# Row differences of a Winograd input transform by accumulating DMAs instead of VectorE subtractions

## The chip, the core and the metric

The kernel runs on one NeuronCore of a Trainium2 chip. TensorE (PE) multiplies matrices and writes its sums to PSUM; VectorE (DVE), ScalarE (ACT) and GpSimd (POOL) work elementwise; SyncE (SP) issues the loads and stores. ScalarE and GpSimd can issue DMAs too. The metric is the device time of one execution in microseconds. Lower is better. The time before is the median of three runs.

## What is computed

A residual block of a diffusion network, in bf16, on an input of 2 images x 512 channels x 64 x 64:

```
def gn(z, gamma, beta):            # group norm, 4 groups of 128 channels
    ...
h = conv3(_silu(gn(x, g1, be1)), w1)          # 3x3 convolution, 512 -> 512
h = h + (_silu(t_emb) @ w_emb).reshape(B, C, 1, 1)
h = conv3(_silu(gn(h, g2, be2)), w2)
return x + h
```

The two 3x3 convolutions are nearly all of the work.

## The kernel before

**Tiling.** Each convolution is one "layer" (0 and 1). A layer is cut into four chunks, (b, ch): two images and, in each, two halves of 32 rows. For each chunk the kernel computes four output tiles `ot` of 128 channels; one (chunk, ot) is called a group here, so there are 16 groups in a layer and 32 in all. The rows go through a Winograd transform F(4,3): six transformed row positions stand for four output rows. Of these positions 0, 5, 3 and 4 take three column taps each ("direct", L670), and positions 1 and 2 are transformed along the columns as well ("nested", L681). A group is thus 24 matmuls into `mid` (positions 3 and 4), 24 into two `acc` banks (positions 0 and 5) and 32 shorter ones into `nst`. The last chunk of layer 1 treats positions 3 and 4 as nested too.

**The input transform** is made by the generator `produce_V` (L374). For each chunk it handles four units, one for each 128 input channels `ct`, so there are 32 units in all. A unit takes these steps:

- SP loads 34 rows (L389), except in the very first chunk, whose image already lies in SBUF.
- ScalarE applies the group norm and SiLU into `a_tmp` (L396), one of two buffers, of 36 rows of 66 columns; GpSimd clears the border row (L383 or L385).
- ScalarE writes 4 times the rows into planes 1 to 4 of `kt` (L408). After this the generator yields.
- VectorE makes the row differences in `kt`: L410, L411 and L412 with 1056 elements in each partition, and L414 with 528. The generator yields again.
- VectorE makes V from `kt`: L428 and two times L437 for the rows, then L448 and two times L453 for the columns.

There is one `kt` tile (`kt_main`). Only the first chunk alternates between two (`kt_two`). So L408 of the next unit has to wait until L437 of this unit has read `kt`.

**The output side of a group.** ScalarE moves `nst` from PSUM into `rm` (L716, twice) and `mid` too (L731). VectorE combines them (L723 to L725, then L738 to L747) into `tt`. In the groups that do not end on VectorE, TensorE adds `tt` into the `acc` banks with two matmuls against a scaled identity (L755), and ScalarE writes the result (L764). This end of a group is issued only after the nested matmuls of the next group. In the groups of `DVE_ENDS` VectorE does it instead (L761). ScalarE also takes the sums for the second group norm (L772, L774) and scales most of the weights (L239), whose transform VectorE finishes (L236); the weights of layer 0 are prepared during its first chunk and those of layer 1 around the boundary of the layers.

**What sets the order.** The program is written by groups, and a small planner (`_Background`) steps the generators of V and of the weights between the matmul sets, by their deadlines. A scheduling layer then orders the instructions on each engine by its own estimate of when each becomes ready. Each engine runs its queue in that order, so that an instruction which waits holds up everything behind it on its engine. GpSimd's queue before holds only memsets of `a_tmp` and the small power operations of the group norm (L174, L176, L181).

Of the kernel before, what the change touches and what calls it, by code (L numbers as in the profile page):

```python
# [9 lines left out]
ACT = mybir.ActivationFunctionType  # L10
ALU = mybir.AluOpType
# [3 lines left out]
F16 = mybir.dt.float16  # L15
# [47 lines left out]
def kernel(  # L63
# [13 lines left out]
    nc = tc.nc  # L77
    P = nc.NUM_PARTITIONS
# [5 lines left out]
    WP = W + 2  # L84
# [3 lines left out]
    TH = 4  # L88
    TR = 8
    CR = TH * TR  # L90
# [4 lines left out]
    EPS = 1e-5  # L95
    WS = 64.0
    KAPPA = 1.0 / (6.0 * WS)
    ROW = TR * WP
    VD, VN = 4 * ROW, NC * 2 * NHALF
    VCT = VD + VN  # L100
    VTMP = 2 * ROW
    NMAT = 14
# [8 lines left out]
    consts = ctx.enter_context(tc.tile_pool(name="consts", bufs=1))  # L111
# [6 lines left out]
    otmp = ctx.enter_context(tc.tile_pool(name="otmp", bufs=1))  # L118
# [24 lines left out]
    a_tmp = [consts.tile([P, CR + 4, WP], F16, name=f"a_tmp{i}") for i in range(2)]  # L143
    for at in a_tmp:
        nc.gpsimd.memset(at[:, :, 0:WP:WP - 1], 0.0)
    kt_main = consts.tile([P, TR, 7, WP], F16, name="kt")

    gparm = consts.tile([4 * CT, P], BF16, name="gparm")
    tparm = consts.tile([B * ET, P], BF16, name="tparm")
# [5 lines left out]
    def flat(t):  # L155
        return t[:].rearrange("p r w -> p (r w)")
# [187 lines left out]
    def new_V():  # L344
        return vpool.tile([P, CT * VCT + VTMP], F16, tag="V", name="V")

    def v_direct(V, ct):
        return V[:, ct * VCT:ct * VCT + VD].rearrange("p (s t w) -> p s t w", s=4, w=WP)

    def v_nested(V, ct):  # L350
        return V[:, ct * VCT + VD:(ct + 1) * VCT].rearrange("p (c q n) -> p c q n", c=NC, q=2)
# [4 lines left out]
    def v_nested34(V, ct, c):  # L356
        if c < 2:
            t = V[:, ct * VCT:ct * VCT + 4 * NHALF]
        else:
            t = more["V"][:, ct * 4 * NHALF:(ct + 1) * 4 * NHALF]  # L360
        return t.rearrange("p (c q n) -> p c q n", c=2, q=2)
# [12 lines left out]
    def produce_V(layer, b, ch, resident=None, V=None, kts=(kt_main,)):  # L374
        if V is None:
            V = new_V()
        Vt[(layer, b, ch)] = V
        r0 = ch * CR - 1
        lo, hi = max(r0, 0), min(r0 + CR + 2, H)
        for ct in range(CT):  # L380
            at, kt = a_tmp[ct % 2], kts[ct % len(kts)]
            if ch == 0:
                nc.gpsimd.memset(at[:, 0, 1:W + 1], 0.0)  # L383
            if ch == NCH - 1:
                nc.gpsimd.memset(at[:, CR + 1, 1:W + 1], 0.0)  # L385
            if resident is None:
                src = srcp.tile([P, CR + 2, W], BF16 if layer == 0 else F16, tag="src")
                src_dram = x_v[b, ct] if layer == 0 else h_scr[b, ct]
                nc.sync.dma_start(  # L389
                    out=src[:, lo - r0:hi - r0, :],  # L390
                    in_=src_dram[:, lo * W:hi * W].rearrange("p (r w) -> p r w", w=W),
                )
                sap = src[:, lo - r0:hi - r0, :]
            else:
                sap = resident[ct][:, lo:hi, :]
            nc.scalar.activation(  # L396
                out=at[:, lo - r0:hi - r0, 1:W + 1], in_=sap,
                func=ACT.Silu, bias=nb_all[:, layer, b, ct:ct + 1],
                scale=sc_all[:, layer, b, ct:ct + 1],
            )  # L400

            def rows(j, n):
                return at[:, j:j + CR, :].rearrange("p (t f) w -> p t (f w)", f=TH)[:, :, 0:n * WP]

            def planes(j, n):
                return kt[:, :, j:j + n].rearrange("p t f w -> p t (f w)")

            nc.scalar.activation(out=planes(1, 4), in_=rows(0, 4), func=ACT.Copy, scale=4.0)  # L408
            yield
            nc.vector.tensor_tensor(out=planes(5, 2), in0=planes(3, 2), in1=planes(1, 2), op=ALU.subtract)  # L410
            nc.vector.tensor_tensor(out=planes(2, 2), in0=planes(2, 2), in1=rows(3, 2), op=ALU.subtract)  # L411
            nc.vector.tensor_tensor(out=kt[:, :, 1:5:3], in0=at[:, 4:4 + CR].rearrange("p (t f) w -> p t f w", f=TH)[:, :, 0:2],  # L412
                                    in1=at[:, 2:2 + CR].rearrange("p (t f) w -> p t f w", f=TH)[:, :, 0:2], op=ALU.subtract)
            nc.vector.tensor_scalar(out=kt[:, :, 0], in0=kt[:, :, 6], scalar1=0.5, scalar2=None, op0=ALU.mult)  # L414
            yield
            Vc = v_direct(V, ct)
            vt = V[:, CT * VCT:].rearrange("p (q t w) -> p q t w", q=2, w=WP)

            four = (layer, b, ch) == FOUR
            if four:  # L420
                vt2 = stage.tile([P, 2, TR, WP], F16, tag="stage", name="vt2")

            def pair(k):
                s = Vc[:, k].rearrange("p t w -> p (t w)")
                return bass.AP(tensor=s.tensor, offset=s.offset,
                               ap=[list(s.ap[0]), [vt[:, k].offset - s.offset, 2], [1, ROW]])

            nc.vector.tensor_tensor(out=Vc[:, 2:4], in0=kt[:, :, 1:5:3].rearrange("p t f w -> p f t w"),  # L428
                                    in1=kt[:, :, 5:7].rearrange("p t f w -> p f t w"), op=ALU.subtract)
            in0 = kt[:, :, 1:4:2].rearrange("p t f w -> p f t w")  # L430
            in1 = kt[:, :, 0:3:2].rearrange("p t f w -> p f t w")
            for k, op in enumerate((ALU.add, ALU.subtract)):
                if four:
                    for i, o in enumerate((vt2[:, k], vt[:, k])):
                        nc.vector.tensor_tensor(out=o, in0=in0[:, i], in1=in1[:, i], op=op)
                else:
                    nc.vector.tensor_tensor(out=pair(k).rearrange("p q (t w) -> p q t w", w=WP), in0=in0, in1=in1,  # L437
                                            op=op)

            def columns(rows2, lo2, hi2):  # L440
                vrow = rows2.rearrange("p q t w -> p (q t) w")

                def plane_pair(o, step):
                    r = vrow[:, :, o:o + HALF]
                    return bass.AP(tensor=r.tensor, offset=r.offset,
                                   ap=[list(r.ap[0]), list(r.ap[1]), [step, 2], [1, HALF]])

                nc.vector.tensor_tensor(  # L448
                    out=lo2.rearrange("p c q (t w) -> p (q t) c w", w=HALF),
                    in0=plane_pair(0, HALF + 2), in1=plane_pair(1, HALF), op=ALU.subtract)  # L450
                ev, od = vrow[:, :, HALF + 1:W + 1], vrow[:, :, 1:HALF + 1]
                for c, (i0, i1, op) in enumerate(((ev, od, ALU.add), (od, ev, ALU.subtract))):
                    nc.vector.tensor_tensor(out=hi2[:, c].rearrange("p q (t w) -> p (q t) w", w=HALF),  # L453
                                            in0=i0, in1=i1, op=op)

            Vn = v_nested(V, ct)
            columns(vt, Vn[:, 0:2], Vn[:, 2:4])
            yield
            if four:
                columns(vt2[:], v_nested34(V, ct, 0), v_nested34(V, ct, 2))  # L460
# [12 lines left out]
    for i, prm in enumerate((g1, be1, g2, be2)):  # L473
        nc.scalar.dma_start(
            out=gparm[CT * i:CT * (i + 1), :],
            in_=prm.rearrange("(ct p) -> ct p", p=P),
# [42 lines left out]
        me_gram(me[:, 1], b0[:, 0:P])  # L519
        gn_scale_bias(b0, me, 0, 0, ct, 1)  # L520

    kt_two = otmp.tile([P, TR, 7, WP], F16, tag="rm", name="kt_two")
    gen_V0 = produce_V(0, 0, 0, resident=x0_res, V=V0, kts=(kt_main, kt_two))
    def two_banks(ct):
        if ct % 2 == 0:
# [52 lines left out]
    for layer in range(2):  # L578
        for idx, (b, ch) in enumerate(chunks):
            for ot in range(CT):  # L580
# [41 lines left out]
                rows = slice(ch * CR * W, (ch + 1) * CR * W)  # L622

                ssum = ssq = None
                if layer == 1:
                    xr = stg.tile([P, CR, W], BF16, tag="io")
                    nc.sync.dma_start(
                        out=xr[:], in_=x_v[b, ot][:, rows].rearrange("p (r w) -> p r w", w=W))
# [13 lines left out]
                accs = {}  # L642
# [60 lines left out]
                rm = otmp.tile([P, 2, CR * W], F16, tag="rm")  # L703
# [10 lines left out]
                def evac_nested(k=0):  # L714
                    for bank in range(2):
                        nc.scalar.activation(  # L716
                            out=raw[:, bank].rearrange("p q t e w -> p (q t e w)"),
                            in_=accs["nst", k][bank][:].rearrange("p q t e w -> p (q t e w)"), func=ACT.Copy,
                            scale=(KAPPA, 0.5 * KAPPA)[bank])

                def cols_mid(k=0):
                    m1, m2 = raw[:, 1, :, :, 0], raw[:, 1, :, :, 1]
# [7 lines left out]
                def evac_mid():  # L730
                    i_a = nc.scalar.activation(  # L731
                        out=msl[:, 0:4:2].rearrange("p s t w -> p s (t w)"),
                        in_=accs["mid"][:].rearrange("p s t e w -> p s (t e w)"), func=ACT.Copy, scale=KAPPA)
                    if not first_evac:
                        first_evac.append(i_a)

# [172 lines left out]
```

## Time and profile before

| What | Value |
|---|---|
| median of 3 runs | 515.71 us (515.32 to 516.96) |
| the profiled execution | 513.87 us |
| its span, first to last instruction | 512.0 us |
| mean granted TensorE clock | 0.985 |
| PE busy | 487.2 us, 3184 matmuls |
| DVE busy | 445.0 us, 1008 instructions |
| ACT busy | 345.8 us, 351 instructions |
| POOL busy | 16.8 us, 56 instructions |
| DMA | 59.87 MB, of which q1 59.32 MB with 34.7% of 16 engines |

Busy time is the time in which an engine had an instruction running. A row of the groups of instructions gives the line, the engine, the operation, the tiles (out<-in), the shapes (partitions x elements), the count, then busy us and mean ns of one, then the idle time of the engine ahead of it and what ended that idle time. A row of the DMA issues gives the tiles, the queue, the count, the size of one in KB and the median time from issue to landing. The views by stretch give the busy us of each engine in a window of the span, the granted clock, the DMA share and GB/s.

### The profile page before, as it was taken

Reading aid. Unit: us, or ns where it says so; the run is one execution under the profiler, and the core shown is the slowest. Engines: PE = TensorE matmul, PEld = TensorE weight load, DVE = VectorE, ACT = ScalarE, POOL = GpSimd, SP = SyncE. Lnnn points to the kernel's source line nnn. Section 1 sums busy time; section 2 is a strip of 40 time slices with the busy share of each in tenths; the row PEclk is TensorE's granted clock in tenths of the full one; section 3 lists DMA queues with packets and bytes.
Section 4 is the critical chain, followed back from the end, with each engine's and each line's share of the span. In section 5 each row is a group of like instructions: output and inputs, shape, how many; then the busy total and the mean of one; then the engine's idle time right before and its main releaser. Section 6 shows DMA issues by size and latency. Waiting matters only on the chain.

```text
span 512.0 us, 8257 instructions
## 1 busy us (share of the span) xinstructions
PE 487.2 (95%) x3184; PEld 288.1 (56%) x3184; DVE 445.0 (87%) x1008; ACT 345.8 (68%) x351; POOL 16.8 (3%) x56
## 2 busy tenths in 40 slices
PE   4898899899999999999899999999999999999996
PEld 4766655355555555555454555554555555557784
DVE  4899999999956896378799999987999999987876
ACT  4776999999976964487999998339665353113350
POOL 1210000100000000000000000010000000000000
PEclk9689999999999999999999999999999999999999
DMA  8949312322332221134543813224434311222212
GB/s 310 362 153 308 93 58 84 114 96 83 107 108 91 100 72 42 43 125 109 181 119 101 251 64 130 78 83 140 153 114 137 107 45 55 83 92 76 82 42 84
DMA packets 22996, 59.87 MB, mean 117 GB/s; under 512 B 2091, under 2 KB 11435, under 8 KB 22571
## 3 DMA queue, kind: packets, MB, share of 16 engines
q1 hardware_dynamic: 22896, 59.32, 34.7%
q8 instruction: 25, 0.41, 0.3%
q14 instruction: 16, 0.13, 0.1%
q10 hardware_dynamic: 59, 0.01, 0.0%
HBM read 42.54 MB, written 16.78 MB: 116 GB/s over the span
## 4 chain that ended last, share of the span: by engine, by line
PE 29%; DVE 16%; ACT 4%; issue 2%; POOL 0%; DVEq 0%; ACTq 0%
PE acc L670 10%; PE nst L681 10%; PE mid L670 7%; DVE U L236 2%; DVE V L437 2%; ACT S L239 1%; PE half L670 1%; DVE sts L738 1%; DVE kt L410 1%; DVE S L236 1%; DVE V L428 1%; DVE V L453 1%; DVE kt L411 1%; ACT junk L774 1%; DVE V L448 1%
## 5 line engine op out<-in xcount | busy, mean ns | idle before, releaser
L670 PE MATMUL acc<-V,R 128*128 128x512 f16 x744 | 171.2, 386 | 1.2 <-ACT yst L764 1.2
L670 PE MATMUL mid<-V,U 128*128 128x512 f16 x672 | 157.2, 387 | 2.9 <-ACT rm L716 1.6
L670 PEld LDWEIGHTS <-R 128*128 128x128 bf16 x792 | 77.1, 98 | 92.5 <-issue 1.8
L681 PE MATMUL nst<-V,U 128*128 128x256 f16 x1088 | 124.8, 273 | 0.2 <-DVE U L236 0.2
L681 PEld LDWEIGHTS <-U 128*128 128x128 f16 x1120 | 109.5, 98 | 21.2 <-DVE U L236 0.7
L670 PEld LDWEIGHTS <-U 128*128 128x128 f16 x672 | 65.5, 98 | 86.1 <-issue 8.3
L716 ACT ACTIVATE rm<-nst 128x1024 f16<-128x1024 f32 x72 | 72.1, 1019 | 55.1 <-PE nst L681 36.8
L396 ACT ACTIVATE a_tmp<-src,nb_all,sc_all 128x2112 f16<-128x2112 f16 (+1 forms) x28 | 60.1, 2153 | 25.2 <-DVE nb_all L335 11.5
L408 ACT ACTIVATE kt<-a_tmp 128x2112 f16<-128x2112 f16 x30 | 59.0, 1966 | 15.0 <-DVE V L437 7.8
L731 ACT ACTIVATE rm<-mid 128x1024 f16<-128x1024 f32 x28 | 28.7, 1025 | 24.9 <-PE mid L670 24.9
L437 DVE TENSOR_TENSOR V<-kt 128x1056 f16<-128x1056 f16 x52 | 36.6, 704 | 0.7
L410 DVE TENSOR_TENSOR kt<-kt 128x1056 f16<-128x1056 f16 x30 | 21.1, 703 | 11.8 <-ACT kt L408 11.7
L239 ACT ACTIVATE S<-R 128x1536 f16<-128x1536 bf16 (+1 forms) x28 | 31.1, 1168 | 0.0
L774 ACT ACTIVATE junk<-yst 128x2048 f16<-128x2048 f16 x16 | 30.7, 1917 | 0.1
L772 ACT ACTIVATE junk<-yst 128x1024 f16<-128x1024 f16 x16 | 17.0, 1060 | 19.1 <-DVE yst L747 13.0
L236 DVE TENSOR_TENSOR U<-S 128x1536 f16<-128x1536 f16 x32 | 29.7, 950 | 0.0
L723 DVE TENSOR_TENSOR tu<-rm 128x512 f16<-128x512 f16 x36 | 15.1, 420 | 15.6 <-ACT rm L716 15.5
L738 DVE TENSOR_TENSOR sts<-rm 128x1024 f16<-128x1024 f16 x32 | 21.9, 686 | 4.3 <-ACT rm L731 3.5
L453 DVE TENSOR_TENSOR V<-V 128x512 f16<-128x512 f16 x64 | 25.5, 433 | 0.0
L725 DVE TENSOR_TENSOR rm<-tu,rm 128x1024 f16<-128x1024 f16 x36 | 24.7, 686 | 0.6 <-ACT rm L716 0.2
L448 DVE TENSOR_TENSOR V<-V 128x1024 f16<-128x1024 f16 x32 | 22.5, 703 | 0.4
L239 ACT ACTIVATE S<-g1t 128x768 f16<-128x768 bf16 x28 | 22.1, 846 | 0.0
(131 smaller groups left out, 479.9 us busy)
## 6 DMA issues: line engine op xcount, KB each, us to landing
src<-h_scr SPq DMA_DIRECT2D x16, 528.0 KB, 3.9
h_scr<-yst SPq DMA_DIRECT2D x16, 512.0 KB, 2.6
xr<-in_x_dram SPq DMA_DIRECT2D x16, 512.0 KB, 3.8
out_dram<-xr SPq DMA_DIRECT2D x15, 512.0 KB, 2.8
src<-in_x_dram SPq DMA_DIRECT2D x12, 528.0 KB, 6.8
R<-in_w_dram SPq DMA_DIRECT2D x16, 384.0 KB, 3.7
xt<-in_x_dram SPq DMA_DIRECT2D x8, 512.0 KB, 4.7
g1t<-in_w_dram SPq DMA_DIRECT2D x16, 192.0 KB, 2.9
```

Of the source, the lines that this page charges most:

```text
L236: nc.vector.tensor_tensor(out=o, in0=i0, in1=i1, op=op)
L239: ts = lambda o, i, f: nc.scalar.activation(out=o, in_=i, func=ACT.Copy, scale=f)
L396: nc.scalar.activation(out=at[:, lo - r0:hi - r0, 1:W + 1], in_=sap, func=ACT.Silu, bias=nb_all[:, layer, b, ct:ct + 1], scale=sc_all[:, l ...
L408: nc.scalar.activation(out=planes(1, 4), in_=rows(0, 4), func=ACT.Copy, scale=4.0)
L437: nc.vector.tensor_tensor(out=pair(k).rearrange("p q (t w) -> p q t w", w=WP), in0=in0, in1=in1, op=op)
L448: nc.vector.tensor_tensor(out=lo2.rearrange("p c q (t w) -> p (q t) c w", w=HALF), in0=plane_pair(0, HALF + 2), in1=plane_pair(1, HALF), o ...
L453: nc.vector.tensor_tensor(out=hi2[:, c].rearrange("p q (t w) -> p (q t) w", w=HALF), in0=i0, in1=i1, op=op)
L670: nc.tensor.matmul(out, lhsT=w_direct(pos, ct, kx), rhs=rhs, start=first, stop=last)
L681: nc.tensor.matmul(accs["nst", (pos - 1) // 2][bank][:, q, :, plane, :], lhsT=lhsT, rhs=rhs.rearrange("p (t w) -> p t w", w=HALF), start=s ...
L716: nc.scalar.activation(out=raw[:, bank].rearrange("p q t e w -> p (q t e w)"), in_=accs["nst", k][bank][:].rearrange("p q t e w -> p (q t ...
L731: i_a = nc.scalar.activation(out=msl[:, 0:4:2].rearrange("p s t w -> p s (t w)"), in_=accs["mid"][:].rearrange("p s t e w -> p s (t e w)") ...
L774: nc.scalar.activation(out=junk[:], in_=yf, func=ACT.Square, scale=float(HW) ** -0.5, accum_out=ssq[:, ch:ch + 1])
```

## The change

The transform's intermediate planes are laid out anew and their signs turned. `kt` becomes two blocks of four planes. With r0 to r5 the six rows under one tile, block 1 holds T_j = r_(j+2) - 4 r_j for j = 0 to 3, and block 0 holds 2 (r1 - r3) and r2 - r4. ScalarE writes block 1 with scale -4 as one contiguous run of 2112 elements in each partition. The rows r_(j+2) are then added into it:

- in every unit but the four of the first chunk, by two accumulating DMAs from `a_tmp` into `kt`, 1056 elements of each partition apiece, issued by GpSimd;
- in the first chunk by one VectorE addition of 2112 elements.

VectorE keeps one subtraction of 1056 elements and one scaling of 528 in this step. The step that makes V has the same number of instructions with the same shapes, reading other planes. Since two planes of V come out with the opposite sign, the scales at which PSUM is read are negated.

```
+    ROWS_BY_DMA = lambda layer, b, ch: (layer, b, ch) != (0, 0, 0)
...
-    kt_main = consts.tile([P, TR, 7, WP], F16, name="kt")
+    kt_main = consts.tile([P, 2, TR, 4, WP], F16, name="kt")
...
-            nc.scalar.activation(out=planes(1, 4), in_=rows(0, 4), func=ACT.Copy, scale=4.0)
+            whole = kt[:, 1].rearrange("p t f w -> p (t f w)")
+            nc.scalar.activation(out=whole, in_=flat(at)[:, 0:CR * WP], func=ACT.Copy, scale=-4.0)
+            below = flat(at)[:, 2 * WP:(2 + CR) * WP]
+            if ROWS_BY_DMA(layer, b, ch):
+                for h in range(2):
+                    part = slice(h * CR * WP // 2, (h + 1) * CR * WP // 2)
+                    nc.gpsimd.dma_start(out=whole[:, part], in_=below[:, part], accum_op=ALU.add)
             yield
-            nc.vector.tensor_tensor(out=planes(5, 2), in0=planes(3, 2), in1=planes(1, 2), op=ALU.subtract)
-            nc.vector.tensor_tensor(out=planes(2, 2), in0=planes(2, 2), in1=rows(3, 2), op=ALU.subtract)
-            nc.vector.tensor_tensor(out=kt[:, :, 1:5:3], in0=at[:, 4:4 + CR].rearrange("p (t f) w -> p t f w", f=TH)[:, :, 0:2],
-                                    in1=at[:, 2:2 + CR].rearrange("p (t f) w -> p t f w", f=TH)[:, :, 0:2], op=ALU.subtract)
-            nc.vector.tensor_scalar(out=kt[:, :, 0], in0=kt[:, :, 6], scalar1=0.5, scalar2=None, op0=ALU.mult)
+            if not ROWS_BY_DMA(layer, b, ch):
+                nc.vector.tensor_tensor(out=whole, in0=whole, in1=below, op=ALU.add)
+            nc.vector.tensor_tensor(out=planes(0, 0, 2), in0=rows(1, 2), in1=rows(3, 2), op=ALU.subtract)
+            nc.vector.tensor_scalar(out=kt[:, 0, :, 0], in0=kt[:, 0, :, 0], scalar1=2.0, scalar2=None, op0=ALU.mult)
             yield
...
-            nc.vector.tensor_tensor(out=Vc[:, 2:4], in0=kt[:, :, 1:5:3].rearrange("p t f w -> p f t w"),
-                                    in1=kt[:, :, 5:7].rearrange("p t f w -> p f t w"), op=ALU.subtract)
-            in0 = kt[:, :, 1:4:2].rearrange("p t f w -> p f t w")
-            in1 = kt[:, :, 0:3:2].rearrange("p t f w -> p f t w")
+            T4 = kt[:, 1].rearrange("p t f w -> p f t w")
+            nc.vector.tensor_tensor(out=Vc[:, 2:4], in0=T4[:, 2:4], in1=T4[:, 0:2], op=ALU.subtract)
...
+            in0, in1 = both(1, 2), both(0, 1)
...
-                            scale=(KAPPA, 0.5 * KAPPA)[bank])
+                            scale=(-KAPPA, -0.5 * KAPPA)[bank])
...
-                        in_=accs["mid"][:].rearrange("p s t e w -> p s (t e w)"), func=ACT.Copy, scale=KAPPA)
+                        in_=accs["mid"][:].rearrange("p s t e w -> p s (t e w)"), func=ACT.Copy, scale=-KAPPA)
```

More of the change, by code (lines that the diff above doesn't have):

```diff
@@ L403, in rows, with planes @@
                 return at[:, j:j + CR, :].rearrange("p (t f) w -> p t (f w)", f=TH)[:, :, 0:n * WP]
-            def planes(j, n):
-                return kt[:, :, j:j + n].rearrange("p t f w -> p t (f w)")
-            nc.scalar.activation(out=planes(1, 4), in_=rows(0, 4), func=ACT.Copy, scale=4.0)
-            yield
-            nc.vector.tensor_tensor(out=planes(5, 2), in0=planes(3, 2), in1=planes(1, 2), op=ALU.subtract)
-            nc.vector.tensor_tensor(out=planes(2, 2), in0=planes(2, 2), in1=rows(3, 2), op=ALU.subtract)
-            nc.vector.tensor_tensor(out=kt[:, :, 1:5:3], in0=at[:, 4:4 + CR].rearrange("p (t f) w -> p t f w", f=TH)[:, :, 0:2],
-                                    in1=at[:, 2:2 + CR].rearrange("p (t f) w -> p t f w", f=TH)[:, :, 0:2], op=ALU.subtract)
-            nc.vector.tensor_scalar(out=kt[:, :, 0], in0=kt[:, :, 6], scalar1=0.5, scalar2=None, op0=ALU.mult)
+            def planes(k, j, n):
+                return kt[:, k, :, j:j + n].rearrange("p t f w -> p t (f w)")
+            whole = kt[:, 1].rearrange("p t f w -> p (t f w)")
[5 more added lines that the diff above has]
+                    nc.gpsimd.dma_start(out=whole[:, part], in_=below[:, part], accum_op=ALU.add)
+            yield
+            if not ROWS_BY_DMA(layer, b, ch):
+                nc.vector.tensor_tensor(out=whole, in0=whole, in1=below, op=ALU.add)
+            nc.vector.tensor_tensor(out=planes(0, 0, 2), in0=rows(1, 2), in1=rows(3, 2), op=ALU.subtract)
+            nc.vector.tensor_scalar(out=kt[:, 0, :, 0], in0=kt[:, 0, :, 0], scalar1=2.0, scalar2=None, op0=ALU.mult)
             yield
@@ L426, in pair, with both @@
                                ap=[list(s.ap[0]), [vt[:, k].offset - s.offset, 2], [1, ROW]])
-            nc.vector.tensor_tensor(out=Vc[:, 2:4], in0=kt[:, :, 1:5:3].rearrange("p t f w -> p f t w"),
-                                    in1=kt[:, :, 5:7].rearrange("p t f w -> p f t w"), op=ALU.subtract)
-            in0 = kt[:, :, 1:4:2].rearrange("p t f w -> p f t w")
-            in1 = kt[:, :, 0:3:2].rearrange("p t f w -> p f t w")
+            T4 = kt[:, 1].rearrange("p t f w -> p f t w")
+            nc.vector.tensor_tensor(out=Vc[:, 2:4], in0=T4[:, 2:4], in1=T4[:, 0:2], op=ALU.subtract)
+            def both(d, t):
+                o = kt[:, 1, :, t].offset - kt[:, 0, :, d].offset
+                v = kt[:, 0, :, d]
+                return bass.AP(tensor=v.tensor, offset=v.offset,
+                               ap=[list(v.ap[0]), [o, 2]] + [list(e) for e in v.ap[1:]])
+            in0, in1 = both(1, 2), both(0, 1)
             for k, op in enumerate((ALU.add, ALU.subtract)):
@@ L520, in stats0 @@
         gn_scale_bias(b0, me, 0, 0, ct, 1)
-    kt_two = otmp.tile([P, TR, 7, WP], F16, tag="rm", name="kt_two")
+    kt_two = otmp.tile([P, 2, TR, 4, WP], F16, tag="rm", name="kt_two")
     gen_V0 = produce_V(0, 0, 0, resident=x0_res, V=V0, kts=(kt_main, kt_two))
```

## The prediction

> **What bounds the kernel now.** I read the page's busy times first, then TensorE's time by stretch, then who made TensorE wait, then the rows of the instructions that the change touches.
>
> ```profile
> PE 487.2 (95%) x3184; PEld 288.1 (56%) x3184; DVE 445.0 (87%) x1008; ACT 345.8 (68%) x351; POOL 16.8 (3%) x56
> ```
>
> TensorE is busy for 95% of the span, so VectorE's 87% is not the bound by itself. What VectorE can give back is only the time in which TensorE waits for it. The view by stretch shows where that is (columns: window and its length, then busy us of PE, PEld, DVE, ACT and POOL, clock, DMA share, GB/s).
>
> ```profile
> 46.00:130.00 84.00, 79.19 (x508) 45.15 (x506) 81.70 (x176) 77.57 (x89) 3.06 (x9) 1.00 0.32 106
> 130.00:246.00 116.00, 116.00 (x680) 64.37 (x679) 85.47 (x205) 82.77 (x91) 3.00 (x9) 1.00 0.30 94
> 246.00:365.00 119.00, 114.09 (x640) 62.42 (x639) 111.75 (x241) 95.99 (x101) 2.95 (x10) 1.00 0.38 124
> 365.00:503.00 138.00, 138.00 (x853) 83.36 (x852) 126.17 (x276) 57.98 (x51) 0.70 (x4) 1.00 0.25 85
> ```
>
> From 130 to 246 us and from 365 to 503 us TensorE has no gap at all. It idles for 84.00 - 79.19 = 4.8 us in the first stretch and 119.00 - 114.09 = 4.9 us in the third, together 9.7 us. These are the stretches in which VectorE is nearly full (81.70 of 84.00 and 111.75 of 119.00). Ahead of 46 us the first chunk is prepared, which the DMAs do not touch. TensorE's waits after 46 us name the causes:
>
> ```profile
> PE acc L755 <- DVE tt L740: 2.3, 2, 1.7
> PE acc L755 <- DVE tt L742: 1.9, 2, 1.7
> PE mid L670 <- ACT rm L716: 1.6, 1, 1.6
> PE acc L755 <- DVE tt L744: 1.4, 4, 0.7
> PE acc L670 <- ACT yst L764: 1.2, 2, 0.9
> ```
>
> Eight waits at L755, 2.3 + 1.9 + 1.4 = 5.6 us, are for `tt` from VectorE; the rest is mostly ScalarE's. So the change can win at most 9.7 us, and 5.6 us if it only speeds up VectorE.
>
> **What is removed.** These rows bear on it:
>
> ```profile
> L408 ACT ACTIVATE kt<-a_tmp 128x2112 f16<-128x2112 f16 x30 | 59.0, 1966 | 15.0 <-DVE V L437 7.8 <-DVE V L435 6.6 <-DVE var L173 0.6
> L410 DVE TENSOR_TENSOR kt<-kt 128x1056 f16<-128x1056 f16 x30 | 21.1, 703 | 11.8 <-ACT kt L408 11.7
> L411 DVE TENSOR_TENSOR kt<-kt,a_tmp 128x1056 f16<-128x1056 f16 x30 | 21.2, 706 | 0.5
> L412 DVE TENSOR_TENSOR kt<-a_tmp 128x1056 f16<-128x1056 f16 x30 | 21.0, 701 | 0.0
> L428 DVE TENSOR_TENSOR V<-kt 128x1056 f16<-128x1056 f16 x30 | 21.0, 701 | 0.5 <-PE acc L670 0.5
> L453 DVE TENSOR_TENSOR V<-V 128x512 f16<-128x512 f16 x64 | 25.5, 433 | 0.0
> ```
>
> In 28 units two of the three subtractions go: 28 x 2 x 0.70 = 39 us of VectorE, 1.4 us a unit. Of these, units 4 to 10 (counted from 0) lie in the first stretch and units 18 to 25 in the third. In the four units of the first chunk, one addition of 2112 elements takes the place of two of 1056. It is not in the trace: it costs at least one row of L410, 0.70 us, and at most two, 1.41 us. I take 1.23 us, since 544 elements more make L410 0.27 us longer than L453, so 1056 more make 0.70 + 0.52. That is 0.2 us less a unit, under 1 us in all, and counts as nothing beside the open points. ScalarE's copy keeps its 2112 elements; written contiguously it lies between L774's 1.92 us for 2048 and the present 1.97 us, so 0 to -0.05 us a unit. The sign changes are constants of existing instructions and cost nothing.
>
> **What is added: a DMA's latency between ScalarE's copy and VectorE.** In each of the 28 units V's first instruction (L428 before) now waits for two accumulating DMAs. They wait for the copy, are issued one after the other by GpSimd, and together carry 128 x 2112 x 2 bytes = 528 KB of `a_tmp`, and must read the same amount of `kt` before they write it. No row shows an accumulating DMA or one issued by GpSimd. The nearest are:
>
> ```profile
> src<-h_scr SPq DMA_DIRECT2D x16, 528.0 KB, 3.9
> h_scr<-yst SPq DMA_DIRECT2D x16, 512.0 KB, 2.6
> src<-in_x_dram SPq DMA_DIRECT2D x12, 528.0 KB, 6.8
> ...
> g1t<-in_w_dram SPq DMA_DIRECT2D x16, 192.0 KB, 2.9
> ```
>
> From below: the pair lands no faster than the store's 2.6 us with a free issue. From above: the two run one after the other at the slow load's 6.8 us each, 13.6 us, plus two issues. For an issue the longest GpSimd row is L181 with 1.04 us and the shortest a 0.2 us memset; I take 1 us. I take the load of the same 528 KB, 3.9 us, behind two issues, with the second read beside the first: **latency 5.9 us**, ends 2.6 and 15.7 us.
>
> By the Trainium skill (DMA: Bandwidth & Descriptors, section "Anatomy of one DMA") a DMA from GpSimd takes about 2.0 us plus bytes over 436 GB/s, an estimate of 2.6 us for each half, and 3.2 us if the pair overlaps fully; the rows agree on the order of size (2.6 and 3.9 us for about 512 KB). With that the latency would be 4 to 5 us, and the sum below would come out close to no change. The skill's page SBUF — State Buffer, section "Who interferes with whom", speaks against the change: VectorE instructions in a two-port mode shut GpSimd out of SBUF, and so hold up the descriptors of its DMAs. No row of this trace shows it.
>
> **What covers it.** In the timeline of ScalarE and VectorE I took, for each unit, the time from the end of L408 to the start of L428. For units 4 to 10 it is 8.6, 9.1, 4.5, 2.4, 3.1, 3.5 and 2.5 us; for units 18 to 25 it is 2.2, 3.1, 18.5, 17.9, 3.7, 3.4, 3.5 and 4.7 us; in the other 13 it lies between 2.4 and 17.4 us. Relative to before, VectorE is late by latency minus this margin (the 1.4 us that go are inside the margin, so it is early by at most 1.4 us). At 5.9 us the short margins leave it late by 1.2 to 3.7 us, in 11 of those 15 units.
>
> VectorE's queue is in order, so what stands behind the waiting instruction matters. In the built program the waits of units 6, 10, 22 and 25 stand behind the group's `tt` work, and TensorE's L755 is safe. In units 7, 18, 19, 23 and 24 work that frees `rm` or makes `tt` (L723 to L742) stands right behind. Their lateness is 3.5, 3.7, 2.8, 2.5 and 2.4 us, mean 3.0. Units 8 and 9 are alike, but TensorE has no gap from 112 to 130 us, and a group has slack there: from the end of `mid` to L755 lie 24 `acc` and 32 `nst` matmuls, 5.34 + 3.49 = 8.8 us in the chain of waits, against L731's 1.0 us and VectorE's 2.8 us up to L742. That is 5 us, enough for 3.
>
> In the five exposed units TensorE already waits nearby (0.8 us at 104, 2.3 us at 253 to 256, 0.7 us at 346, 0.3 us at 361), so there is no slack. But what stands behind also needs two L716 that stand behind the copy on ScalarE, 2 x 1.02 = 2.0 us, and waits for those anyway. So I charge 3.0 - 2.0 = 1.0 us each: **5 us lost**. The charge could be 3.0 us each, 15 us.
>
> ScalarE's next copy waits for L437 as before, which is now later; between two copies its queue has 6 to 10 us of other work, which hides it at 5.9 us, but not at 10. `a_tmp` is held until the DMAs have read it; there are two buffers, so the next-but-one L396 sees nothing.
>
> GpSimd's queue gets 56 DMA issues. Behind them stand the border memsets, which sit idle for up to 33 us today before they may start, and the group norm's L174 and L181, for which VectorE waited 1.3 us at 92 us. One or two issues ahead of these cost up to 2 us there; I take 1 us.
>
> The data adds to the DMA engines: 28 x 528 KB read twice and written once. They are 30 to 38% busy in these stretches and not the bound; slower loads hide behind the two `src` buffers.
>
> **What is won.** The DVE waits at L755 away from exposed units shrink, as do ScalarE's waits behind VectorE: of the 9.7 us I take 2 us.
>
> **Sum.** 5 + 1 - 2 = +4 us. The profiled execution's 513.87 us becomes 517.9. It lies 1.84 us under the median of the runs, so the forecast is 519.7 us.
>
> **The rivals.**
>
> - *The DMAs land in time (faster).* If the latency is under about 4 us, most margins cover it, and VectorE's 1.4 us a unit come through in the stretches where it is full. Up to 5.6 us of L755 waits and some of ScalarE's go: 6 us at most likely, 509.7 us. For it: 23 of the 28 margins reach 4.5 us once the 1.4 us that go are added. Against: the load of this size alone takes 3.9 us, without issue and accumulation. It decides at a latency of 4.5 us.
> - *The latency is 9 us or more (much slower).* Then all units with margins of 2 to 5 us put VectorE and ScalarE's next copy late by 4 to 7 us, past the 5 us slack as well. Charging 1 to 2 us in some 12 units gives +12 to +18 us, 528 to 534 us. For it: read, add and write may run as two passes, and loads in flight take up to 6.8 us.
> - *Nothing moves.* TensorE bounds at 95%, and the waits that come equal those that go: 515.7 us, within 0.3%, which is about what a measurement of this kernel can tell from no change. It also holds if VectorE's relief is real but each L755 then waits for ScalarE.
>
> **Chances.** Forecast (a few us slower) 0.38, much slower 0.16, nothing moves 0.12, faster 0.34. This makes faster 0.34, within 0.3% 0.12, slower 0.54. Cases of both signs hold most of it: the forecast's own range is 517.3 to 525 us. The range for 8 in 10 reaches from the faster rival's 509 to 530 us, where the charge of 3.0 us in each exposed unit (+15 us, 529.7) ends.
>
> **What would show it.** VectorE's busy time should fall by about 39 us, to 406. L428's successor should show idle time ended by a DMA, some 1 to 4 us in each of about 20 units. TensorE's idle in 46 to 130 us and 246 to 365 us should grow, from 9.7 to about 14 us, at L755 and at `nst` or `mid` waiting for ScalarE; the two gapless stretches should stay gapless. The time from the copy's end to that instruction shows the latency. The prediction is wrong if it is under 4.5 us, or if the waits fall where VectorE would have been idle anyway.

## The result

The changed kernel takes 556.82 us (median of 4 runs, 555.08 to 558.54) against 516.17 us (515.32 to 516.96): 1.079 times as long, with a 95% interval of 1.076 to 1.082. Forecast were 519.7 us and at most 530. The profiled execution took 556.5 us, its span is 554.7 us, the mean granted clock 0.963.

### The profile page after: what moved, and what is told of

Its sections match the earlier page's. It is cut to its first block, busy times and chain, and to the rows that moved or that the text cites. A ratio compares the mean times of both kernels' runs of the same rounds, so it can differ in the third digit from the quotient of the medians.

```text
span 554.7 us, 8343 instructions
## 1 busy us (share of the span) xinstructions
PE 500.5 (90%) x3184; PEld 291.8 (53%) x3184; DVE 414.4 (75%) x948; ACT 346.3 (62%) x351; POOL 65.5 (12%) x112
## 3 DMA queue, kind: packets, MB, share of 16 engines
q0 software_dynamic: 8064, 15.14, 15.8%
## 4 chain that ended last, share of the span: by engine, by line
PE 22%; DMA 22%; ACT 20%; DVE 18%; issue 13%; POOL 4%; ACTq 0%; DVEq 0%; SPq 0%; POOLq 0%
DMA kt<-a_tmp 20%; PE acc L682 8%; PE nst L693 7%; ACT kt L410 7%; PE mid L682 4%; ACT a_tmp L397 4%; ACT rm L728 3%; DVE U L237 3%; POOL kt L415 2%; ACT S L240 2%; DVE V L449 2%; ACT yst L776 1%; DVE V L435 1%; ACT junk L786 1%; DVE sts L750 1%
## 5 line engine op out<-in xcount | busy, mean ns | idle before, releaser
L682 PE MATMUL mid<-V,U 128*128 128x512 f16 x672 | 162.6, 396 | 2.8 <-DVE V L449 1.6
L693 PE MATMUL nst<-V,U 128*128 128x256 f16 x1088 | 129.4, 278 | 11.1 <-DVE U L237 5.7
L693 PEld LDWEIGHTS <-U 128*128 128x128 f16 x1120 | 111.0, 99 | 35.6 <-DVE U L237 7.6
L682 PEld LDWEIGHTS <-U 128*128 128x128 f16 x672 | 67.0, 100 | 88.6 <-issue 14.3
L728 ACT ACTIVATE rm<-nst 128x1024 f16<-128x1024 f32 x72 | 71.4, 1018 | 50.4 <-PE nst L693 26.0
L397 ACT ACTIVATE a_tmp<-src,nb_all,sc_all 128x2112 f16<-128x2112 f16 (+1 forms) x28 | 60.0, 2152 | 60.4 <-DMA kt<-a_tmp 42.6
L415 POOL DMA_DIRECT2D kt<-a_tmp x56 | 50.0, 1053 | 273.5 <-ACT kt L410 273.5
L410 ACT ACTIVATE kt<-a_tmp 128x2112 f16<-128x2112 f16 x30 | 58.8, 1961 | 31.3 <-DVE V L449 20.0
L435 DVE TENSOR_TENSOR V<-kt 128x1056 f16<-128x1056 f16 x30 | 21.2, 707 | 60.0 <-DMA kt<-a_tmp 50.0
L735 DVE TENSOR_TENSOR tu<-rm 128x512 f16<-128x512 f16 x36 | 15.2, 422 | 31.7 <-ACT rm L728 31.4
L449 DVE TENSOR_TENSOR V<-kt 128x1056 f16<-128x1056 f16 x52 | 36.6, 704 | 0.7
L743 ACT ACTIVATE rm<-mid 128x1024 f16<-128x1024 f32 x28 | 28.6, 1020 | 10.8 <-PE mid L682 10.8
L240 ACT ACTIVATE S<-R 128x1536 f16<-128x1536 bf16 (+1 forms) x28 | 31.3, 1165 | 0.5 <-DVE U L237 0.5
L750 DVE TENSOR_TENSOR sts<-rm 128x1024 f16<-128x1024 f16 x32 | 22.0, 687 | 12.7 <-ACT rm L743 12.6
L786 ACT ACTIVATE junk<-yst 128x2048 f16<-128x2048 f16 x16 | 30.6, 1913 | 0.2
L767 PE MATMUL acc<-tt,id_end 128*128 128x512 f16 x36 | 12.6, 404 | 19.1 <-DVE tt L756 9.5
L737 DVE TENSOR_TENSOR rm<-tu,rm 128x1024 f16<-128x1024 f16 x36 | 24.7, 687 | 0.7 <-ACT rm L728 0.2
## 6 DMA issues: line engine op xcount, KB each, us to landing
h_scr<-yst SPq DMA_DIRECT2D x16, 512.0 KB, 3.4
xr<-in_x_dram SPq DMA_DIRECT2D x16, 512.0 KB, 4.3
out_dram<-xr SPq DMA_DIRECT2D x15, 512.0 KB, 2.6
xt<-in_x_dram SPq DMA_DIRECT2D x8, 512.0 KB, 4.3
```

The source lines that it names most:

```text
L240: ts = lambda o, i, f: nc.scalar.activation(out=o, in_=i, func=ACT.Copy, scale=f)
L397: nc.scalar.activation(out=at[:, lo - r0:hi - r0, 1:W + 1], in_=sap, func=ACT.Silu, bias=nb_all[:, layer, b, ct:ct + 1], scale=sc_all[:, l ...
L410: nc.scalar.activation(out=whole, in_=flat(at)[:, 0:CR * WP], func=ACT.Copy, scale=-4.0)
L415: nc.gpsimd.dma_start(out=whole[:, part], in_=below[:, part], accum_op=ALU.add)
L682: nc.tensor.matmul(out, lhsT=w_direct(pos, ct, kx), rhs=rhs, start=first, stop=last)
L693: nc.tensor.matmul(accs["nst", (pos - 1) // 2][bank][:, q, :, plane, :], lhsT=lhsT, rhs=rhs.rearrange("p (t w) -> p t w", w=HALF), start=s ...
```

## The profile after

Lines moved by up to twelve: L396 is now L397, L408 is L410, L428 is L435, L437 is L449, L716 is L728, L723 to L725 are L735 to L737, L731 is L743, L738 to L747 are L750 to L759, L755 is L767; the DMAs are L415. First the page's busy times:

```profile
PE 500.5 (90%) x3184; PEld 291.8 (53%) x3184; DVE 414.4 (75%) x948; ACT 346.3 (62%) x351; POOL 65.5 (12%) x112
```

VectorE has lost 30.6 us of work. TensorE's idle time, span minus busy, rose from 512.0 - 487.2 = 24.8 us to 554.7 - 500.5 = 54.2 us, and the same 3184 matmuls take 13.3 us more: 29.4 + 13.3 = 42.7 us, the growth of the span (554.7 - 512.0). By stretch (columns as before):

```profile
46.00:130.00 84.00, 75.21 (x475) 43.12 (x474) 66.61 (x145) 68.28 (x77) 12.87 (x20) 0.96 0.50 133
130.00:246.00 116.00, 111.80 (x641) 60.76 (x640) 73.17 (x182) 79.81 (x87) 15.23 (x25) 0.99 0.47 117
246.00:365.00 119.00, 108.14 (x592) 58.02 (x590) 97.01 (x204) 92.93 (x103) 13.53 (x21) 0.99 0.55 150
365.00:503.00 138.00, 123.91 (x664) 66.79 (x664) 105.09 (x235) 58.04 (x47) 16.47 (x24) 0.95 0.45 119
```

The two stretches that had no gap now have 4.2 and 14.1 us of it, and the last one holds 664 matmuls where it held 853. The granted clock, 1.00 in all four before, is 0.96, 0.99, 0.99 and 0.95 now: 0.04 x 84 + 0.01 x 116 + 0.01 x 119 + 0.05 x 138 = 12.6 us at full clock are missing, about the 13.3 us by which the matmuls took longer. What was waited for (engine, line, releaser: us in all, times, longest):

```profile
DVE V L435 <- DMA kt<-a_tmp: 50.0, 20, 5.3
ACT a_tmp L397 <- DMA kt<-a_tmp: 42.6, 11, 7.0
DVE tu L735 <- ACT rm L728: 31.4, 15, 5.6
...
ACT kt L410 <- DVE V L449: 20.0, 8, 7.8
...
DVE V L435 <- ACT rm L728: 9.9, 2, 5.4
...
PE acc L767 <- DVE tt L756: 9.5, 5, 4.0
PE acc L767 <- DVE tt L752: 9.1, 4, 5.3
```

Besides GpSimd's border memset two engines wait for the DMAs: VectorE at V's first instruction, and ScalarE at L397, because it may not overwrite `a_tmp` until a DMA has read it. The two waits of L435 that are put down to L728, in units 4 and 17, were for DMAs too: the pairs landed 11.8 and 7.4 us behind the copy's end, and V started 0.1 to 0.2 us later. So VectorE lost 59.9 us in 22 units. One passage of the timeline (start, us, engine, line, ..., idle before) shows both, from unit 26:

```profile
399.55 1.98 ACT L410 ACTIVATE kt<-a_tmp 128x2112 f16<-128x2112 f16 x1
401.41 1.04 ACT L743 ACTIVATE rm<-mid 128x1024 f16<-128x1024 f32 x1
409.47 2.15 ACT L397 ACTIVATE a_tmp<-src,nb_all,sc_all 128x2112 f16<-128x2112 f16 x1 [7.03 <-DMA kt<-a_tmp]
```

```profile
404.43 0.42 DVE L754 TENSOR_TENSOR tt<-qs,sts 128x512 f16<-128x512 f16 x1
409.38 0.71 DVE L435 TENSOR_TENSOR V<-kt 128x1056 f16<-128x1056 f16 x1 [4.54 <-DMA kt<-a_tmp]
410.01 0.68 DVE L756 TENSOR_TENSOR tt<-tt,xr 128x1024 f16<-128x1024 f16 x1
```

```profile
403.67 3.66 PE L693 MATMUL nst<-V,U 128*128 128x256 f16 x32
410.75 0.66 PE L767 MATMUL acc<-tt,id_end 128*128 128x512 f16 x2 [3.42 <-DVE tt L756]
411.20 2.34 PE L682 MATMUL mid<-V,U 128*128 128x512 f16 x5
```

The copy ends at 401.53 us and L435 starts at 409.38, 7.85 us later. Behind L435 in VectorE's queue stands L756, which TensorE needs, so TensorE stands idle for 3.42 us. ScalarE idles for 7.03 us at the SiLU of unit 28, with the copy of unit 27 queued behind it. And the five matmuls after the gap take 2.34 us, 0.47 us each, where 24 of them took 5.50 us, 0.23 us each; the granted clock was 0.50 from 411.40 to 413.54 us.

## The experiments

Runs with an interval are medians of several; the others are one run each, read beside the kernel before on the same chip (515.4 to 516.6 us). An edit "VectorE adds" sets `ROWS_BY_DMA` to false.

**Without the DMAs.** `ROWS_BY_DMA = lambda layer, b, ch: False`

> The new layout stays, but VectorE adds the 2112 elements in every unit, as the changed kernel does in the first chunk; there is no DMA. If the time comes from the DMAs (the wait at L435, a_tmp held until they have read it, or their traffic), it returns to the time before or a little under it: VectorE spends 1.25 us on the addition where it spent 2 x 0.70 us, 0.15 us a unit less, so 511 to 517 us. If the new layout and the order of instructions that comes with it cost the time, it stays above 535 us.

Measured: 518.56 us, 1.0055 (1.0027 to 1.0082). So 38 of the 41 us come from the DMAs. The new layout and order cost about 2.8 us, a little over the range expected; which instruction makes them was not settled.

**DMAs in one layer only.** `... layer == 0 and (b, ch) != (0, 0)`, and `... layer == 1`

> The DMAs add the rows only in layer 0, in the 12 units of its last three chunks; VectorE adds them elsewhere. TensorE's idle time grew by 8.2 us from 46 to 246 us (4.8 to 13.0 us) and by about 20 us from 246 to 503 us (4.9 to 25.0 us), and 13 us went to slower matmuls in all. If the cost is local, unit by unit, this kernel keeps a third of the 41 us: 527 to 533 us, and the time here and of the kernel with the DMAs in layer 1 alone add up to the whole. If the DMAs hurt by one bad place only (a load that delays unit 4 until 57.7 us), it keeps nearly all or nearly nothing.

> The DMAs add the rows only in layer 1, in its 16 units; VectorE adds them in layer 0. If the cost is local, it keeps about two thirds of the 41 us, 539 to 546 us. If the weights of layer 1, prepared around the boundary, and the DMAs hurt each other only there, the rest of layer 1 is as before and the time is under 530 us.

Measured: 530.02 and 541.92 us, both as expected. Over 518.56 they cost 11.5 us in 12 units and 23.4 us in 16, together 34.8 of 38.3. The cost is spread out, about 1.0 us a unit in layer 0 and 1.5 in layer 1.

**Plain copies.** `dma_start(out=whole[:, part], in_=below[:, part])`, without `accum_op`

> The same two DMAs of the same size from the same queue, but as plain copies without accumulation: it leaves out the term of -4 times the rows, so V is not the transform. If reading, adding and writing back makes the latency, the pair lands 1.5 to 2.5 us sooner than 5.5 us behind the copy and the time falls by more than half of the 41 us, to 525 to 537 us. If the latency is that of the issue and of a transfer of this size, it stays within 5 us of 557.

Measured: 523.24 us, a little below the range of the first theory: only 4.7 us over the kernel without DMAs. From the DMA issues and the groups of this kernel:

```profile
kt<-a_tmp POOLq DMA_DIRECT2D x56, 264.0 KB, 2.7
```

```profile
L415 POOL DMA_DIRECT2D kt<-a_tmp x56 | 31.2, 558 | 277.2 <-ACT kt L410 276.6
```

The same two views of the changed kernel:

```profile
kt<-a_tmp POOLq DMA_DIRECT2D x56, 264.0 KB, 4.5
```

```profile
L415 POOL DMA_DIRECT2D kt<-a_tmp x56 | 50.0, 1053 | 273.5 <-ACT kt L410 273.5
```

In both traces each engine runs its instructions in the same order, so the order of the queues does not make the difference. Adding makes an issue 1.05 us instead of 0.56 and the landing 4.5 us instead of 2.7. From the copy's end to V's first instruction the shortest times are 3.7 and 5.5 us. These 1.8 us cost 33.6 us: VectorE's wait at L435 is 21.8 us in 10 units with plain copies and 50.0 in 20 with adding ones, and ScalarE's at L397 25.2 and 42.6 us.

**Half by DMA.** One DMA for the second half, VectorE adds the first.

> VectorE adds the first half of the rows (1056 elements, about 0.70 us) and one accumulating DMA the second half, so the chain behind the copy is shorter by one issue: some 4.5 us in place of 5.5. If the time goes by the latency, it lies between the plain copies (3.7 us of latency, 523.2 us) and the changed kernel (5.5 us, 556.8 us): 530 to 545 us. If it goes by how much is accumulated, half the 38 us remain, 537 us, which this run does not tell from it; if by the presence of any accumulating DMA, it stays above 550 us.

Measured: 531.13 us, with the wait at L435 at 29.0 us (17 times), landings of 3.7 us and no wait of L397 for the DMAs. It lies between, as the latency says; with 12.6 of the 38.3 us left it is also not far from half, so this run does not tell the latency from the amount that is accumulated.

**Traffic without waits.** `dma_start(out=spare[:, part], in_=<weights>, accum_op=add)` behind the copy, VectorE adds.

> Two staging buffers; VectorE adds the rows in every unit, and in 24 units GpSimd issues the same two accumulating DMAs of the same size behind the copy, but from a weight tile into a spare tile that nobody reads. If issue, traffic or GpSimd's queue cost the time, it stays above 530 us. If only the waits for the DMAs cost it, it is within 4 us of the kernel in which VectorE does all additions, 511 to 520 us.

Measured: 521.58 us, 1.6 us over the range, and 3.0 us over the kernel without DMAs, with 24 of the 28 pairs in flight and landing in 4.3 us. The two staging buffers may be part of the 3.0 us. So issue and traffic explain 3 of the 38 us at most; in this kernel neither VectorE nor ScalarE waits for a landing.

**Which wait.** Two staging buffers free the memory; `a_tmp` in three, or `kt` in two:

> The changed kernel with two staging buffers for weights instead of three, so that there is memory for the next three kernels; nothing else differs. All theories: within 4 us of 557; it is the base for the kernels beside it.

> Two staging buffers as in the base beside it, and three a_tmp buffers in turn instead of two. ScalarE's L397 waited 42.6 us for the DMAs to have read a_tmp. If that wait, in order ahead of the evacuations, makes most of the time, L397's wait for DMAs falls under 5 us and the time falls by 15 to 30 us, to 527 to 542 us. If VectorE's own wait at L435 (50.0 us) makes it, the time stays within 6 us of the base.

> Two staging buffers, and two kt in turn, so that ScalarE's copy L410 need not wait until VectorE has made V of the unit before (31.3 us of waits in the changed kernel, 15.0 before). If that wait carries VectorE's lateness on, the time falls by 8 to 20 us. If a_tmp's is what blocks ScalarE, it moves by under 5 us, since the next SiLU waits for the DMA anyway.

Measured: base 561.38, three `a_tmp` 551.53 (-9.9), two `kt` 546.21 us (-15.2). With three `a_tmp` L397's wait fell only from 44.9 to 30.4 us, not under 5, and the gain lies between the two expectations. With two `kt`, ScalarE's wait for V at its copy fell from 24.7 to 3.5 us and L435's from 54.0 to 28.5. So both buffers carry the latency on, `kt` more than `a_tmp`, and neither alone is the cause. Both together were not tried.

**One unit ahead.** Copy and DMAs of unit ct + 1 are written ahead of VectorE's work on unit ct, with two `kt`; and the control where VectorE adds.

```
for ct in range(CT):
    for c in range(ct, min(ct + 2, CT)): heads.setdefault(c, head(c))
```

> Two staging buffers and two kt, and the load, the SiLU, the copy and the DMAs of a unit are written one unit ahead, before VectorE's work on the unit before. Now the DMAs have some 10 us. If the waits for the DMAs are the whole cost, VectorE's wait at its first instruction of V falls under 10 us in all, and the time falls to that of the kernel beside it, in which VectorE adds in the same order, or 2 to 6 us below it. If the cost is in a_tmp being held or in the traffic, the time stays above 530 us.

> The control: the same order one unit ahead, two staging buffers and two kt, but VectorE adds the rows in all units and there are no DMAs of rows. All theories: 514 to 526 us, from 518.6 us with the old order and up to 4.6 us for the two staging buffers.

> The order one unit ahead, two kt, two staging buffers, VectorE adds in all units, no DMA of rows: the same as the control that had 515.5 us in one run, timed. 513 to 518 us: within 0.3% of the kernel before, or up to 0.5% faster, since two kt take ScalarE's waits for VectorE away.

Measured: 534.56 us with DMAs; 515.51 us in one run and 515.82 us timed for the control, 1.000 (0.998 to 1.002). Of the DMAs' cost half remains, 534.56 - 515.5 = 19 us. Two `kt` alone gave 546.21 us, so the lead by itself takes off 11.7 us. The expectation that L435's wait would fall under 10 us failed: it is still 37.4 us, in 11 units. The control shows that this order with two `kt` takes back the 2.8 us of the new layout, and does not beat the kernel before.

**Only where the margin is long.**

> DMAs in six units only, those in which ScalarE's copy ends 9 to 20 us before V's first instruction when VectorE adds (units 4, 5, 12 to 13, 20, 21 and 28 to 29 without their neighbours: the first unit of the second chunk of each image, in both layers, and the second for the first image). If a DMA costs only where its 5.5 us are not covered, these cost nothing and VectorE gains 1.25 us each: 515 to 519 us, the same as or a little under the 518.6 us with no DMA. If each DMA costs by itself, 38 us over 28 units is 1.4 us a unit, and six make 8 us: 526 us.

Measured: 525.52 us, 1.017 (1.012 to 1.022). The six units were 4, 5, 12, 20, 21 and 28. The expectation of the latency theory failed, so they were split.

> DMAs in units 4 and 5 only, the first two of the second chunk of layer 0, while the loads of weights and of x run. If the late landing under these loads (11.7 us behind the copy in the changed kernel) makes the cost of the six units, it is all here: 523 to 527 us. If every DMA costs by itself, it is 2 x 1.2 us: 521 us.

> DMAs in units 12, 20 and 21 only (the first unit of the last chunk of layer 0, the first two of the second chunk of layer 1), VectorE adds elsewhere. If a DMA costs only where its landing is late, these three cost nothing: 516 to 520 us, as with no DMA (518.6 us). If every DMA costs by itself, 7 us over six units is 1.2 us each: 522 us.

Measured: units 4 and 5 alone 522.62 us, 1.0126 (1.009 to 1.016), half a microsecond short of the 523 us expected; units 12, 20 and 21 alone 520.21 us, 1.0072 (1.005 to 1.009), which can't be told from the 1.0055 without DMAs. The two differ in the landing. Unit 4's two DMAs landed 8.5 and 10.4 us behind their issues, unit 5's 3.3 and 4.9 us; from 47 to 58.3 us, while unit 4's were in flight beside loads of weights and x, the DMA engines were 93% busy. GpSimd's queue in the run of the two units:

```profile
47.01 2.00 POOL L415 DMA_DIRECT2D kt<-a_tmp  x2 [5.99 <-ACT kt L410]
58.19 0.15 POOL L386 MEMSET a_tmp<- 128x64 f16 x1 [9.18 <-DMA kt<-a_tmp]
```

The pair issued by 49.01 us has read `a_tmp` only at 58.2. TensorE in the same run:

```profile
59.42 0.39 PE L693 MATMUL nst<-V,U 128*128 128x256 f16 x2 [1.99 <-DVE U L237]
59.65 1.04 PE L682 MATMUL mid<-V,U 128*128 128x512 f16 x3
63.26 3.17 PE L693 MATMUL nst<-V,U 128*128 128x256 f16 x14 [2.58 <-DVE U L237]
66.22 2.07 PE L682 MATMUL mid<-V,U 128*128 128x512 f16 x7
68.13 1.69 PE L693 MATMUL nst<-V,U 128*128 128x256 f16 x14
```

It waits for weights, which VectorE transforms behind its wait for the DMA: 1.99 + 2.58 us, where the kernel without DMAs has 0.4 us of such waits from 46 to 95 us. The 14 `nst` matmuls behind the second wait take 3.17 us instead of 1.69. The granted clock (the third number from the end) had fallen before that wait began:

```profile
55.00:60.00 5.00, 3.01 (x27) 2.35 (x25) 1.68 (x3) 4.06 (x6) 0.15 (x1) 1.00 0.63 177
60.50:66.50 6.00, 3.42 (x16) 2.26 (x16) 5.93 (x12) 4.31 (x4) 1.79 (x2) 0.50 0.21 38
67.00:70.00 3.00, 3.00 (x22) 2.06 (x21) 3.00 (x8) 1.75 (x3) 0.15 (x1) 1.00 0.76 148
```

**The best places together.** One unit ahead, DMAs in twelve units:

> The order one unit ahead with DMAs in twelve of the 28 units, those in which V's first instruction came 11 us or more behind the copy and did not wait for the DMA (three of the last chunk of layer 0, and four, two and three of the last three chunks of layer 1). If only landings that are waited for cost, VectorE gains 12 x 1.25 = 15 us and loses nothing: 511 to 516 us, at or under the control of the same order. If the new order of instructions or the shared queues bring the waits back, 517 to 525 us.

Measured: 519.29 us, 1.0074 (1.005 to 1.010), 3.5 us over its control. VectorE's busy time is 427.8 us in the profiled runs instead of 440.4, 12.6 us less, and V's first instruction waits for a DMA only once, for 3.1 us; ScalarE's SiLU waits for one three times, 5.6 us. So VectorE's 12.6 us bought no net time even where nearly every landing was hidden. Whether they are worth nothing, or less than the waits that are left, this run does not tell apart.

**What stands behind the wait.** `with tc.high_priority():` around the evacuations and `tu`, `sts`, `tt`

> The changed kernel, with the evacuations of nst and mid and VectorE's end of a group (tu, sts, tt) given precedence over the transform in the order of the queues. Where unit 26 had the tt instructions that TensorE needs right behind the waiting instruction of V, they now stand ahead of it. If what stands behind the waiting instructions makes the cost, the time falls by 8 to 25 us, to 532 to 549 us. If VectorE's and ScalarE's lost time itself makes it, it moves by under 5 us from 557 us.

> The control: the same precedence with VectorE adding in all units. All theories: 513 to 521 us, within 1% of the time with VectorE's additions in the old order, since there is no long wait to be moved past.

Measured: 568.25 us with DMAs, 1.101 (1.095 to 1.106); the control 518.61 us, 1.0065. Both theories miss: it is 11 us slower than the changed kernel, not faster. The waits in this kernel:

```profile
DVE V L435 <- DMA kt<-a_tmp: 66.7, 21, 8.8
ACT a_tmp L397 <- DMA kt<-a_tmp: 48.0, 14, 5.1
...
PE acc L767 <- DVE tt L752: 5.7, 5, 2.4
...
PE acc L767 <- DVE tt L756: 3.5, 3, 2.2
```

TensorE's waits for `tt` did fall, from the changed kernel's 9.1 + 9.5 to 5.7 + 3.5 us in these two rows. But VectorE waits 16.7 us longer at L435. A likely reason, not tested by itself, is that the order of precedence took other work from the time that covers the latency. Taking instructions out from behind the wait did not help.

## Why the prediction was wrong

The direction was right and the size was not: +4 us forecast, +41 measured. By its own steps:

- **What bounds.** Right: TensorE. VectorE's relief could win little; no run shows a gain from it (the twelve units above), where 2 us were counted as won and the faster rival had 6.
- **What is removed.** Right: the groups of VectorE's instructions sum to 510.6 us before and 472.0 after, 38.6 us less for the 39 forecast. The page's busy time fell by only 30.6 us, not to 406, because back-to-back instructions overlap in it and there are fewer of those now. The first chunk's addition takes 1.25 us (1.23). But the new layout was not free: 2.8 us.
- **The latency.** Right in size: 5.9 us taken, 5.5 to 8.2 us from the copy's end to V where V waited, 12.0 in unit 4 behind the loads; 1.05 us an issue (1 us). It is partly luck: the 3.9 us in the sum are a plain load of 528 KB, and an accumulating half of 264 KB took 4.5 us. The estimate of 2.6 us for a half, from the Trainium skill (DMA: Bandwidth & Descriptors, section "Anatomy of one DMA"), fits the plain copy's 2.7 us, not the accumulating DMA's 4.5. In Collectives: The Full Stack, section "The bandwidth ceiling: the fold count and why AG ≠ RS ≠ AR", the skill says of the reduce step of a collective that the add needs two source reads and so two descriptors for a chunk where a copy needs one. The packets of GpSimd's queue point the same way here, 8064 against 4480 (1.8 times) for the same 15.14 MB, and 15.8% of the engines' time against 7.7%.
- **The first step that failed: "`a_tmp` is held until the DMAs have read it; there are two buffers, so the next-but-one L396 sees nothing".** L397 waited 42.6 us, 11 times. The queue puts the SiLU of the unit after next soon behind the copy, sometimes right behind it, ahead of evacuations, so the in-order ScalarE passes the latency on. With three `a_tmp` 9.9 us went.
- **The second: "between two copies its queue has 6 to 10 us of other work, which hides it at 5.9 us".** ScalarE's idle time ahead of the copy, nearly all of it for V, grew from 15.0 to 31.3 us, and two `kt` took 15.2 us off.
- **The third: the charge of 1.0 us in five units.** It left out the 13 units of the gapless stretches, although their margins were as short as 2.4 us, because TensorE had no gap there: "the two gapless stretches should stay gapless". No gap says that slack was enough before, not how much there is. They got 18.3 us of TensorE's 29.4 us of new idle time (some of it is the shift of work between windows). In the two stretches that were charged, idle time rose from 9.7 to 19.7 us, not to 14. The five units that were charged waited 1.4, 3.4, 0.4, 3.2 and 3.2 us at VectorE, 11.6 us of the 59.9; the other 17 units that waited were charged nothing. And no sum over units at one engine would do, since the wait comes again at ScalarE.
- **GpSimd's queue, charged 1 us.** VectorE's wait for the group norm's last power operation grew from 4.0 to 4.6 us, about as charged.
- **Not seen at all:** the lower granted clock after gaps, 13.3 us more of TensorE's busy time.

The ends of ScalarE's move of `mid`, one in each of the first 28 groups, show where the time came from (us behind the kernel before, in the profiled executions; 0.2 to 2.3 us of it stand there already at the copy of unit 4, ahead of the first DMA):

| group | VectorE adds | plain copies | units 4, 5 only | all DMAs |
|---|---|---|---|---|
| 0 | 0.8 | 3.8 | 2.5 | 0.9 |
| 7 | 0.9 | 7.1 | 7.3 | 14.5 |
| 12 | 1.5 | 4.9 | 7.9 | 17.0 |
| 19 | 0.9 | 4.4 | 8.5 | 22.0 |
| 22 | -0.6 | 9.7 | 6.5 | 38.6 |
| 27 | 1.8 | 9.3 | 9.0 | 42.7 |

With all DMAs the loss comes in steps, at units 4 and 5, in groups 5 to 8, and above all in groups 20 to 24 of layer 1. Of the rivals, "much slower" named the right mechanism, V and the next copy late together, but tied it to 9 us of latency; it happened at 5.5 to 8.2 us. Between plain and adding DMAs the profiled spans differ by 33.3 us; 7.1 us of it are slower matmuls (PE busy 493.4 and 500.5 us), the rest is idle time of TensorE. What stays open is how that idle time splits between VectorE's queue and ScalarE's: each wait could be lessened alone, none was removed with the others in place. Open too is how much the order adds: with DMAs the scheduling layer orders the queues anew (unit 5's copy ends at 63.3 us, before at 77.9), and the prediction read its margins in the old order.

## What to carry to other kernels

A DMA that takes the place of an instruction on a chain of engines puts its whole latency between them, and each buffer that it reads or writes makes another in-order engine wait: list those buffers, and ask of each who comes next for it. Count the margin in every unit, also where the bounding engine has no gap, for a gapless stretch says nothing of its slack. And first ask whether the relief is worth anything: here VectorE was 87% busy, and taking work from it bought no net time even where the DMA was nearly hidden.

## What the hardware showed

- An accumulating DMA costs GpSimd 1.05 us to issue and lands in 4.5 us for 264 KB (SBUF to SBUF); the plain one 0.56 and 2.7 us. A border memset right behind such issues takes 0.67 us on average (L384), behind plain ones 0.17 us, and its like elsewhere 0.15 us (L386).
- The granted clock of TensorE can fall to half after a short gap. In the run of units 4 and 5 it was 0.50 from 60.5 to 66.5 us, where 14 `nst` matmuls took 3.17 instead of 1.69 us; the gap ahead of the fall was 1.99 us, and the gap of 2.58 us came after it. In the changed kernel it was 0.50 behind the 3.42 us, and five `mid` matmuls took 2.34 instead of some 1.15 us. The length of the gap alone does not decide: after 1.57 us and 1.69 us in the kernel before, speed was as ever (14 in 1.69 us, 24 in 5.50 us), and after a wait of 3.3 us for ScalarE's L776 in the kernel without DMAs the clock stayed at 1.00.
- The Trainium skill (TensorE: Matmul & The Clock Gate, section "HAM oscillation — how this bites in real kernels") gives "no PE-idle gaps >~3.4µs." as the rule. Here a gap of 1.99 us was enough, and the measurement decides.
